# Attention: a pair's query and key copies queued behind the last exponential two pairs ahead, loads half a pair sooner

## The chip, the cores and the metric

The kernel runs on one core of one Trainium2 chip. The metric is the device time of one execution in microseconds (us). The engines are named as the profile names them: PE (TensorE, matrix products), PEld (its weight loads), DVE (VectorE), ACT (ScalarE), POOL (GpSimd) and SP (SyncE, which issues the DMAs here). Each engine works through its own queue in order.

## The reference

A causal attention feeds two mixture-of-experts style layers. Only the attention part is touched by the change.

```
batch, n_heads, seq, head_dim = (2, 12, 448, 64)
scale = 1.0 / np.sqrt(q.shape[-1])
scores = scale * np.matmul(q, k.transpose(0, 1, 3, 2))
mask = np.triu(np.ones((seq, seq), dtype=bool), k=1)
scores = np.where(mask, -1000000000.0, scores)
scores = scores - np.max(scores, axis=-1, keepdims=True)
attn = np.exp(scores)
attn = attn / (np.sum(attn, axis=-1, keepdims=True) + 1e-09)
return np.matmul(attn, v).astype(np.float32)
...
x = np.ascontiguousarray(attn_out.transpose(0, 2, 1, 3)).reshape(B * S, H * D)
x = _moe_ref(x=x, **moe_kwargs)
return _moe2_ref(x=x, **moe2_kwargs)
```

## The kernel before

**Pairs.** The 24 heads are handled as 12 pairs (`units`, numbered `u` from 0): two heads of 64 dimensions fill the 128 partitions. Matrix products keep float32 accuracy by splitting each operand into a high and a low part and adding three products: high by high, high by low, low by high.

**Preparing a pair (`s_prep`, L179).** `kh` is the key's high part (a DVE copy, L62), `kl` its low part (a POOL subtraction, L67). `qs` holds the scaled query, high part from ACT (L60), low part from a DVE instruction (L191, `SCALAR_TENSOR_TENSOR`). From the second pair on, `qs` is then copied by two DMAs on SP's queue (L202, one per head) into the block layout `q` with zeros between the heads. There are two `q` buffers (`qz`), so pair u and pair u+2 share one; three raw buffers `qk` for the loads (`s_load`, L171), and two raw buffers `v` (`load_v`, L177).

**Scores and softmax.** Per pair there are seven chunks of 64 query rows (c = 0 to 6, 64(c+1) key columns). A chunk is three products on PE (L229, tile `s`, four buffers in PSUM), a masked maximum on DVE (L239, tile `mn`) and an exponential on ACT (L242, tile `p`, with row sums). POOL scales `p` by the reciprocal sums (`s_norm`, L246; `rs` is the sums' tile), PE transposes it (L272, tile `pt`), ACT and DVE make its high and low part, PE multiplies by the values (L290, tile `pv`), and ACT and DVE make the high and low part of the result (`xhi`, `xlo`).

**The loop.** The loop over half pairs (k from -3; `u, h = divmod(k, 2)`) writes PE's order out by hand in `products`. An odd half k = 2u+1 holds pair u's transposes 2 and 3, the scores of pair u+2 for the chunks 2, 0, 1, 3 and value products of pair u-1. The even half k = 2u holds the scores of pair u+1 for the chunks 6, 4, 5, pair u's transposes 0 and 1 and value products. So a pair's scores begin with chunk 2 in an odd half and end with chunk 5 in the next even one. On the other engines the order is the scheduler's; `tc.issue_after(x)` tells it to put an instruction behind x. In the kernel before, the preparation of pair u+3 is written in the odd half k = 2u+1, behind the maximum and the exponential of chunk 1 of pair u+2. Near the end of the attention, the first products of the next layer (`pa`, L314 to L316) are mixed in; their weights are converted on DVE (L118 to L122) and POOL.

At the start of the program, `warm` issues dummy products (`wp`, six at first) while the first loads come in.

Of the kernel before, what the change touches and what calls it, by code (L numbers as in the profile page):

```python
# [32 lines left out]
def f32(ap):  # L33
    return ap.bitcast(F32)


CFG = dict(
    first=1, rt5=[1, 3, 4, 5, 8], hp=3000, xe=[1, 7, 8, 10, 12], turn=5, xfd=[3, 4, 5, 6], xfj=[1, 2, 3, 4],
    joint=1, mhi="A", rt6=[1, 4, 7, 9, 15], woh="A", h2h="A", h2l="V", rt=[1, 3, 5, 7, 10], et=[9, 10, 14],
    turn2=[1, 3], ft0=[(0, 3), (1, 3), (2, 3), (3, 3), (4, 3)], ft1=[4], ft2=[3, 5, 6, 7], late=[(2, 5), (3, 5)], ew=[2, 4, 10, 10, 10, 12, 14], stop=0, mlo="V", xh="A", h2="A",  # L40
    wh="G", wil="G", wol="GV", warm=6, nsa=6, nwi=3, nwb=3, wo0=4, hs0=[4, 5, 8, 9], conv0=17, convs=2, pin=1,
    qsb=2, pb=2, ptb=2, qkraw=3, vraw=2, vb=2, ss=4, pts=2, pvs=2, pas=4, wsp=1,
    man=(2, 21),
    ch=(((2, 0, 1), (3,), ()), ((6,), (4, 5), ())), wn=[3, 2, 2], qh="A", qdir=1, qss=2, rpin=5, qdma="SS", kh="V",
    vh="AG", kl="G", vl="G", pth="AAAA", nrm="GGGGGGG", u0=1, order=[2, 1, 3, 0, 4], pm=1,
# [3 lines left out]
def build(tc, qkd, vd, w_in, w_out, emb, tau, wm, cst, out, dbg_y=None):  # L49
    nc = tc.nc  # L50
    V, A, G, T, DMA = nc.vector, nc.scalar, nc.gpsimd, nc.tensor, nc.sync

    ENG = {"A": A, "V": V, "G": G, "S": DMA}
# [4 lines left out]
    def copy_on(eng, out, in_, scale=1.0):  # L58
        if eng is A:
            return A.activation(out, in_, AF.Copy, scale=scale)  # L60
        elif scale == 1.0:
            return eng.tensor_copy(out, in_)  # L62
        else:
            return eng.tensor_scalar(out=out, in0=in_, scalar1=scale, scalar2=None, op0=ALU.mult)

    def lo_of(eng, lo, x, hi):
        return eng.tensor_tensor(out=lo, in0=x, in1=hi, op=ALU.subtract)  # L67
# [18 lines left out]
    ct = cpool.tile([P, cs.shape[1]], F32, name="ct")  # L86
# [41 lines left out]
    last = {}  # L128
# [5 lines left out]
    units = [(b, pr) for b in range(B) for pr in range(NP_)]  # L134
    NU = len(units)
# [24 lines left out]
    def ab(key, u):  # L160
        x = CFG[key]
        return ENG[x[units.index(u) % len(x)]]

    def s_load(u):
        b, pr = u
        qk = apool.tile([P, 2, S], F32, tag="qk", bufs=CFG["qkraw"], name="qk")
        if u == units[0]:
            for i in range(2):
                DMA.dma_start(out=qk[:, i], in_=qkd[b, pr, :, i])
        else:  # L170
            DMA.dma_start(out=qk, in_=qkd[b, pr])  # L171
        st[u] = dict(q=qk[:, 0], k=qk[:, 1])

    def load_v(u):
        b, pr = u
        st[u]["v"] = v = apool.tile([P, NB, P], F32, tag="v", bufs=CFG["vraw"], name="v")
        last["load"] = last["load", units.index(u)] = DMA.dma_start(out=v, in_=vd[b, pr])  # L177

    def s_prep(u):  # L179

        d = st[u]
        for x in ("kh", "kl"):
            d[x] = apool.tile([P, S], F32R, tag=x, bufs=CFG["qsb"], name=x)
        d["q2"] = qz[units.index(u) % len(qz)]
        first = u == units[0] and CFG["u0"]
        kh = copy_on(V if first else ab("kh", u), d["kh"], d["k"])

        def split(r, hi, lo):
            q = d["q"][r].rearrange("p (c a) -> p c a", a=QC)
            copy_on(ENG[CFG["qh"]], hi, q, scale=SCALE)  # L190
            V.scalar_tensor_tensor(out=lo, in0=q, scalar=SCALE, in1=f32(hi), op0=ALU.mult, op1=ALU.subtract)  # L191

        heads = [slice(h * D, (h + 1) * D) for h in range(2)]
        if units.index(u) < CFG["qdir"]:
            with tc.issue_after(kh.ins):
                for h, r in enumerate(heads):
                    split(r, d["q2"][r, :, h, :, 0], d["q2"][r, :, h, :, 1])
        else:
            q = apool.tile([P, NQ, QC, 2], F32R, tag="qs", bufs=CFG["qss"], name="qs")
            split(slice(0, P), q[:, :, :, 0], q[:, :, :, 1])  # L200
            for h, r in enumerate(heads):
                ENG[CFG["qdma"][h]].dma_start(out=f32(d["q2"][r, :, h]), in_=f32(q[r]))  # L202
        lo_of(V if first else ab("kl", u), d["kl"], d["k"], f32(d["kh"]))

    def s_prep_v(u):
        d = st[u]
        d["vh"], d["vl"] = vz[units.index(u) % len(vz)]
        vh, vl = (x[:, :, 0:3:2, :] for x in (d["vh"], d["vl"]))
        v = d["v"].rearrange("p a (h b) -> p a h b", h=2)
        copy_on(ab("vh", u), vh, v)  # L210
        lo_of(V if u == units[0] and CFG["u0"] else ab("vl", u), vl, v, f32(vh))
# [119 lines left out]
    def w_in_load():  # L331
        f = len(wt)
        if f < NF:
            wt[f] = w_load(w_in, f, slots[f % NWI], f"wi{f}", wl="wil", parts=CFG["wsp"] if in_attn else 1)

    def norm_at(k):
        u = (k + 2) // 2
        if 0 <= u < NU:
            s_norm(units[u], sum(CFG["ch"][k % 2], ()))
# [2 lines left out]
    s_load(units[1])  # L342
    load_v(units[0])
    s_load(units[2])
    load_v(units[1])
    s_prep(units[0])


# [4 lines left out]
    def warm(n):  # L353
        for _ in range(n):
            T.matmul(wp, wz[:, 0:P], wz, start=True, stop=True)
# [7 lines left out]
    def half_unit(k):  # L363

        u, h = divmod(k, 2)
        run = {}
        for x in (6, 4, 5) if h == 0 else (2, 0, 1, 3):
            v = u + 1 + h
            if 0 <= v < NU:
                run["s", x] = s_scores(units[v], x)  # L370
        if 0 <= u < NU:
            for i in (0, 1) if h == 0 else (2, 3):
                run["t", i] = trans(units[u], i)
        if 1 <= u <= NU:
            for j, g in ((0, 1), (3, 1), (0, 0), (3, 0)) if h == 0 else ((1, 0), (2, 0), (1, 1), (2, 1)):
                run["v", j, g] = s_pv(units[u - 1], j, g)
        return run
# [7 lines left out]
    def products(k, run):  # L385

        h = k % 2
        if h == 0:
            mix(run, ("s", 6))
            mix(run, ("t", 0))  # L390
            mix(run, ("v", 0, 1), ("v", 3, 1), ("v", 0, 0))
            mix(run, ("s", 4))
            mix(run, ("s", 5))
            mix(run, ("v", 3, 0))
            mix(run, ("t", 1))
        elif k == -3:
            mix(run, *(("s", c) for c in (2, 0, 1, 3)))
        else:
            mix(run, ("t", 2))
            mix(run, ("s", 2))  # L400
            mix(run, ("s", 0), ("v", 1, 0))
            mix(run, ("s", 1), ("v", 2, 0))
            mix(run, ("v", 1, 1))
            mix(run, ("v", 2, 1))
            mix(run, ("t", 3))
            mix(run, ("s", 3))

    man_a = tc.manual_schedule(engines={mybir.EngineType.PE})
    for k in range(-3, 2 * NU + 2):
        u, h = divmod(k, 2)  # L410
        if h == 1 and 3 <= u + 4 < NU:
            s_load(units[u + 4])
        if h == 0 and 0 <= u and u + 2 < NU:
            load_v(units[u + 2])
        if k == 2:
            DMA.dma_start(out=ct, in_=cst)
        while len(wt) < min(NWI, max(0, (k - CFG["conv0"]) // CFG["convs"])):
            if CFG["pin"]:
                with tc.issue_after(last["max"].ins):
                    w_in_load()  # L420
            else:
                w_in_load()
        if k == CFG["man"][0]:
            man_a.__enter__()
        if k == CFG["man"][1]:
            man_a.__exit__(None, None, None)
        if k == -3:
            s_prep(units[1])
        norm_at(k)
        products(k, half_unit(k))  # L430
        if k + 3 < len(CFG["wn"]):
            warm(CFG["wn"][k + 3])
        if (k == -2 or h == 1 and u >= 0) and u + 3 < NU:
            i = max(u + 3, 2)
            x = (0, 3) if i == 2 else (i - 1, 1)
            with tc.issue_after(last["max", *x].ins), tc.issue_after(last["exp", *x].ins):
                s_prep(units[i])
        if h == 1 and 0 <= u + 1 < NU:
            with tc.issue_after(last["max", 0, 5].ins), tc.issue_after(last["exp", 0, 5].ins):
                s_prep_v(units[u + 1])  # L440
# [898 lines left out]
```

## Time and profile before

| | before |
|---|---|
| median of 3 runs | 582.53 us (582.45 to 583.53) |
| the profiled execution | 584.23 us, of which the span from first to last instruction is 582.4 us |
| PE busy | 548.3 us (94%) |
| DVE busy | 401.0 us (69%) |
| ACT busy | 290.2 us (50%) |
| POOL busy | 182.7 us (31%) |
| mean granted PE clock | 0.98 |

The attention takes about the first 125 us of the span. In the rest PE is busy almost without a break. A time in the rows is counted from the start of the span. "Idle before" is the idle time of an engine just before an instruction, with what ended it.

### The profile page before, as it was taken

How to read it: one execution, taken by the hardware profiler on the slowest of the kernel's cores; microseconds unless marked ns; L12 is line 12 of the kernel's file. 1: busy time of each engine (PE TensorE's matmuls, PEld its weight loads, DVE VectorE, ACT ScalarE, POOL GpSimd, SP SyncE). 2: the span in 40 equal slices, each digit the busy share in tenths (PEclk: the TensorE clock that was granted, in tenths of full speed). 3: DMA queues.
4: the chain of work that ended last, by engine and by line, in shares of the span. 5: the costliest groups of instructions: out<-in, count | busy, mean ns of one | idle time of the engine just before them, and what ended most of it. 6: DMA issues, size and time to landing. Idle time of an engine off the chain costs nothing.

```text
span 582.4 us, 9627 instructions
## 1 busy us (share of the span) xinstructions
PE 548.3 (94%) x3427; PEld 511.4 (88%) x3428; DVE 401.0 (69%) x956; ACT 290.2 (50%) x638; POOL 182.7 (31%) x228
## 2 busy tenths in 40 slices
PE   7788786899999999999999999999999999999993
PEld 5687786888899999999999999989998898899992
DVE  6867686596488797779565446798267899883641
ACT  4867576552353524442423331851166888764641
POOL 8747575594463565322100000100210201200010
PEclk9989898799999999999999999999999999999997
DMA  7536534232253544633100002910778789874310
GB/s 233 137 108 218 135 87 95 51 110 99 75 194 130 209 162 163 216 135 140 54 1 29 27 28 87 401 56 2 280 236 282 251 288 333 308 238 175 110 50 6
DMA packets 28234, 86.52 MB, mean 149 GB/s; under 512 B 2822, under 2 KB 13062, under 8 KB 28176
## 3 DMA queue, kind: packets, MB, share of 16 engines
q1 hardware_dynamic: 26640, 79.51, 41.3%
q0 software_dynamic: 1536, 6.29, 3.0%
q8 instruction: 29, 0.48, 0.3%
q14 instruction: 29, 0.24, 0.1%
HBM read 75.24 MB, written 6.29 MB: 140 GB/s over the span
## 4 chain that ended last, share of the span: by engine, by line
PE 83%; DMA 6%; DVE 5%; ACT 2%; issue 2%; SPq 1%; POOL 0%; POOLq 0%; DVEq 0%; ACTq 0%
PE yps L577 19%; PE ops L947 10%; PE pa L314 7%; PE pa L315 7%; PE pa L316 7%; DMA q<-qs 5%; PE pv L290 5%; PE s L229 5%; PE hps L848 3%; PE ops L885 2%; PE ops L880 2%; PE hps L866 2%; PE pt L272 2%; PE hps L868 2%; PE hps L867 2%; DVE ml L67 2%
## 5 line engine op out<-in xcount | busy, mean ns | idle before, releaser
L67 DVE TENSOR_TENSOR ml<-xraw,mh 128x768 fp32r<-128x768 f32 x64 | 59.7, 957 | 10.3 <-ACT mh L60 9.5
L229 PE MATMUL s<-kh,q 128*128 128x128 f32 (+6 forms) x168 | 48.6, 336 | 19.3 <-DMA q<-qs 16.8
L242 ACT ACTIVATE p<-s,mn 128x192 f32<-128x192 f32 (+6 forms) x84 | 39.7, 475 | 34.8 <-DVE mn L239 22.2
L60 ACT ACTIVATE mh<-xraw 128x768 fp32r<-128x768 f32 x64 | 52.2, 843 | 7.6 <-PE ops L880 5.8
L229 PEld LDWEIGHTS s<-kh,q 128*128 128x128 f32 x168 | 35.0, 226 | 23.3 <-issue 11.0
L947 PE MATMUL ops<-mh,act 128*128 128x384 f32 x224 | 53.5, 341 | 0.0
L290 PE MATMUL pv<-pt,v 128*128 128x448 f32 (+7 forms) x288 | 51.8, 314 | 0.0
L239 DVE CUSTOM_DVE_ANT_0 s<-s,maskf 128x192 f32<-128x192 f32 (+6 forms) x77 | 32.1, 432 | 26.8 <-PE s L229 25.8
L255 POOL TENSOR_SCALAR p<-p,rs 128x192 f32<-128x192 f32 (+6 forms) x84 | 43.8, 538 | 17.9 <-DVE rs L251 14.4
L122 DVE SCALAR_TENSOR_TENSOR w<-raw,w 128x768 int32<-128x768 int32 x32 | 43.5, 1363 | 0.7
L290 PEld LDWEIGHTS pv<-pt,v 128*128 128x128 f32 (+1 forms) x288 | 42.1, 177 | 1.7
L973 POOL DMA_INDIRECT out<-osb,fsi x10 | 10.3, 1028 | 99.3 <-ACT osb L968 65.9
L947 PEld LDWEIGHTS ops<-mh,act 128*128 128x128 f32 x224 | 39.2, 188 | 0.8
L67 DVE TENSOR_TENSOR hs<-h,hs 128x512 fp32r<-128x512 f32 (+1 forms) x32 | 21.8, 690 | 23.9 <-ACT hs L60 23.8
L67 DVE TENSOR_TENSOR ml<-mraw,mh 128x768 fp32r<-128x768 f32 x32 | 29.9, 956 | 10.2 <-ACT mh L60 9.8
L120 DVE SCALAR_TENSOR_TENSOR w<-raw,w 128x768 int32<-128x768 int32 x32 | 36.5, 1142 | 0.7
L985 POOL DMA_INDIRECT xr<-ydram,fgi x10 | 10.5, 1051 | 84.1 <-DVE fsi L693 45.4
L67 DVE TENSOR_TENSOR pt<-pt 128x512 fp32r<-128x512 f32 x48 | 32.1, 682 | 4.7 <-ACT pt L60 4.4
L320 ACT ACTIVATE relu<-pa 128x448 f32<-128x448 f32 x32 | 17.0, 539 | 35.3 <-PE pa L316 35.3
L118 DVE TENSOR_SCALAR w<-raw 128x768 int32<-128x768 int32 x32 | 23.7, 741 | 12.2 <-POOL wi3l L67 4.2
L60 ACT ACTIVATE pt<-pt 128x512 fp32r<-128x512 f32 x48 | 28.2, 597 | 7.1 <-PE pt L272 7.1
L272 PE MATMUL pt<-ident,p 128*128 128x128 f32 x192 | 28.9, 282 | 0.8 <-DVE pt L67 0.4
(462 smaller groups left out, 1643.5 us busy)
## 6 DMA issues: line engine op xcount, KB each, us to landing
xraw<-in_wm SPq DMA_DIRECT2D x32, 768.0 KB, 6.8
raw<-in_w_in SPq DMA_DIRECT2D x16, 768.0 KB, 5.1
raw<-in_w_out SPq DMA_DIRECT2D x16, 768.0 KB, 4.0
mraw<-in_wm SPq DMA_DIRECT2D x16, 768.0 KB, 6.5
qk<-in_qkd SPq DMA_DIRECT2D x11, 448.0 KB, 5.0
q<-qs SPq DMA_DIRECT2D x22, 224.0 KB, 3.4
v<-in_vd SPq DMA_DIRECT2D x12, 256.0 KB, 3.1
ydram<-ysb SPq DMA_DIRECT2D x7, 384.0 KB, 2.3
```

The lines of the kernel that those rows point to most:

```text
L60: return A.activation(out, in_, AF.Copy, scale=scale)
L67: return eng.tensor_tensor(out=lo, in0=x, in1=hi, op=ALU.subtract)
L122: V.scalar_tensor_tensor(out=w[:, x], in0=raw[:, x, 0], scalar=29, in1=w[:, x], op0=ALU.logical_shift_right, op1=ALU.bitwise_or)
L229: T.matmul(ss, d["q2"][:, c, :, :, x].rearrange("p a b -> p (a b)"), d[y][:, :n], start=i_ == 0, stop=i_ == 2 and not first)
L255: G.tensor_scalar(out=p, in0=p, scalar1=rs[:, COL[c]:COL[c] + 1], scalar2=1.0, op0=ALU.mult, op1=ALU.mult)
L272: T.transpose(pt[:, o * P:(o + 1) * P], d["p"][c][:, j * P:(j + 1) * P], ident)
L290: T.matmul(d["pv"][:, j * P:S] if h else d["pv"][0:D, j * P:S], d[x][:, j, 1:3].rearrange("p a b -> p (a b)") if h else d[x][:, j, 0], pt[ ...
L314: T.matmul(ps, wh[:, c], xhi[:, kc, gs], start=(kc == 0), stop=False)
L315: T.matmul(ps, wh[:, c], xlo[:, kc, gs], start=False, stop=False)
L316: T.matmul(ps, wl[:, c], xhi[:, kc, gs], start=False, stop=(kc == KC - 1))
L577: T.matmul(ps[t][c][:, :384], x, w[:, c * 384:(c + 1) * 384], start=(f == 0 and w is wh and x is hi), stop=(f == NF - 1 and x is lo))
L947: T.matmul(ps[c], x, ww[:, c * 384:(c + 1) * 384], start=(fc == 0 and x is hh and ww is wh), stop=(fc == 7 and x is hl))
```

## The change

The preparation of pair u+3 is written half a pair sooner: in the even half k = 2u, behind the maximum and the exponential of chunk 5 of pair u+1, which is the last use of the `q` buffer that the new pair takes over. The raw query and key load of pair u+4 moves from the odd half k = 2u+1 to the even half k = 2u. The values of pair 1 and the raw load of pair 3 are put behind the first DMA copies of `qs`; the constants' table `ct` goes from k = 2 to k = 3 and behind the values of pair 3. Eight instead of six dummy products stand at the start.

```diff
-    wh="G", wil="G", wol="GV", warm=6, nsa=6, nwi=3, nwb=3, wo0=4, hs0=[4, 5, 8, 9], conv0=17, convs=2, pin=1,
+    wh="G", wil="G", wol="GV", warm=8, nsa=6, nwi=3, nwb=3, wo0=4, hs0=[4, 5, 8, 9], conv0=17, convs=2, pin=1,
...
-                ENG[CFG["qdma"][h]].dma_start(out=f32(d["q2"][r, :, h]), in_=f32(q[r]))
+                last["q"] = ENG[CFG["qdma"][h]].dma_start(out=f32(d["q2"][r, :, h]), in_=f32(q[r]))
...
     s_load(units[2])
-    load_v(units[1])
     s_prep(units[0])
...
-        if h == 1 and 3 <= u + 4 < NU:
-            s_load(units[u + 4])
-        if h == 0 and 0 <= u and u + 2 < NU:
-            load_v(units[u + 2])
-        if k == 2:
-            DMA.dma_start(out=ct, in_=cst)
+        if k == -2:
+            with tc.issue_after(last["q"].ins):
+                load_v(units[1])
+                s_load(units[3])
+        elif h == 0:
+            if u + 4 < NU:
+                s_load(units[u + 4])
+            if u + 2 < NU:
+                load_v(units[u + 2])
+        if k == 3:
+            with tc.issue_after(last["load", 3].ins):
+                DMA.dma_start(out=ct, in_=cst)
...
-        if (k == -2 or h == 1 and u >= 0) and u + 3 < NU:
-            i = max(u + 3, 2)
-            x = (0, 3) if i == 2 else (i - 1, 1)
+        if h == 0 and u + 3 < NU:
+            x = (0, 3) if u < 0 else (u + 1, 5)
             with tc.issue_after(last["max", *x].ins), tc.issue_after(last["exp", *x].ins):
-                s_prep(units[i])
+                s_prep(units[u + 3])
```

What moves on ACT is seen around the exponentials of one pair in mid-attention (`p1c` is chunk c of an odd pair, `p0c` of the next, even one; `qs` is the high part of a coming pair's query). Before:

```order
L242 ACTIVATE p15_125,sm_734<-s_832,mn_735 128x384
L60 ACTIVATE pt_855<-pt_857 128x512
L242 ACTIVATE p02_115,sm_864<-s_867,mn_865 128x192
L242 ACTIVATE p00_113,sm_864<-s_873,mn_865 128x64
L242 ACTIVATE p01_114,sm_864<-s_882,mn_865 128x128
L60 ACTIVATE qs_915<-qk_718 128x448
```

and now:

```order
L242 ACTIVATE p15_125,sm_745<-s_836,mn_746 128x384
L60 ACTIVATE qs_855<-qk_665 128x448
L60 ACTIVATE pt_866<-pt_868 128x512
L242 ACTIVATE p02_115,sm_875<-s_878,mn_876 128x192
L242 ACTIVATE p00_113,sm_875<-s_884,mn_876 128x64
L242 ACTIVATE p01_114,sm_875<-s_893,mn_876 128x128
```

`qs` stood behind the exponential of the next pair's chunk 1, and stands now right behind the last exponential of the odd pair, with one `pt` copy and three exponentials behind it.

On DVE, at the same place of the program, the low part of `qs` (L191) is the instruction that SP's copies wait for; `ISA s,mn` is a masked maximum, whose number of columns tells the chunk (192 is chunk 2, 64 chunk 0, 128 chunk 1, 256 chunk 3, 448 chunk 6). Before:

```order
L67 TENSOR_TENSOR pt_938<-pt_971,pt_937 128x512
L239 ISA s_1003,mn_995<-s_1003,maskf_127 128x64
L239 ISA mn_995 128x1
L239 ISA s_1012,mn_995<-s_1012,maskf_127 128x128
L239 ISA mn_995 128x1
L62 CAST kh_1042<-qk_848 128x448
L251 RECIPROCAL rs_866<-rs_866 128x3
L67 TENSOR_TENSOR pt_986<-pt_987,pt_985 128x512
L239 ISA s_1036,mn_995<-s_1036,maskf_127 128x256
L239 ISA mn_995 128x1
L191 SCALAR_TENSOR_TENSOR qs_1045<-qk_848,qs_1045 128x448
```

and now:

```order
L239 ISA s_966,mn_876<-s_966,maskf_127 128x384
L239 ISA mn_876 128x1
L62 CAST kh_982<-qk_795 128x448
L251 RECIPROCAL rs_877<-rs_877 128x4
L67 TENSOR_TENSOR pt_942<-pt_975,pt_941 128x512
L239 ISA s_1008,mn_1006<-s_1008,maskf_127 128x192
L239 ISA mn_1006 128x1
L239 ISA s_1014,mn_1006<-s_1014,maskf_127 128x64
L239 ISA mn_1006 128x1
L191 SCALAR_TENSOR_TENSOR qs_985<-qk_795,qs_985 128x448
```

`kh` has moved from behind chunk 1's maximum to behind the last maximum of the pair before, and `qs` from behind chunk 3's maximum (in other pairs before: from behind chunk 1's or chunk 6's) to behind chunk 0's.

On POOL the subtraction `kl` is moved too. Before, around the scaling of one even pair's `p`:

```order
L250 TENSOR_SCALAR rs_866<-sm_864 128x4
L67 TENSOR_TENSOR v11_112<-v_663,v10_111 128x4x2x64
L255 TENSOR_SCALAR p02_115<-p02_115,rs_866 128x192
L255 TENSOR_SCALAR p00_113<-p00_113,rs_866 128x64
L255 TENSOR_SCALAR p01_114<-p01_114,rs_866 128x128
L255 TENSOR_SCALAR p03_116<-p03_116,rs_866 128x256
L250 TENSOR_SCALAR rs_866<-sm_864 128x3
L67 TENSOR_TENSOR kl_1043<-qk_848,kh_1042 128x448
```

and now:

```order
L250 TENSOR_SCALAR rs_877<-sm_875 128x4
L67 TENSOR_TENSOR kl_983<-qk_795,kh_982 128x448
L255 TENSOR_SCALAR p02_115<-p02_115,rs_877 128x192
L255 TENSOR_SCALAR p00_113<-p00_113,rs_877 128x64
L255 TENSOR_SCALAR p01_114<-p01_114,rs_877 128x128
L255 TENSOR_SCALAR p03_116<-p03_116,rs_877 128x256
L250 TENSOR_SCALAR rs_877<-sm_875 128x3
```

`kl`, which needs `kh`, now stands ahead of the scaling of the chunks 2, 0, 1 and 3.

## Rows read from the trace of the kernel before

**Rows 1.** PE's waits from 20 to 126 us: total us, times, longest.

```profile
PE s L229 <- DMA q<-qs: 16.8, 8, 3.4
PE s L229 <- ACT p L242: 1.0, 1, 1.0
```

**Rows 2.** Busy us per engine in stretches: pairs, their sum, start and tail; PEclk is granted clock.

```profile
core 0: us, PE busy (x) PEld busy (x) DVE busy (x) ACT busy (x) POOL busy (x), PEclk, DMA share, GB/s
...
20.55:30.41 9.86, 6.46 (x49) 5.84 (x49) 7.07 (x24) 6.78 (x22) 8.26 (x18) 0.99 0.43 106
30.41:40.42 10.01, 9.26 (x61) 8.85 (x62) 6.49 (x21) 6.35 (x19) 4.78 (x8) 0.84 0.35 80
40.42:49.73 9.31, 7.80 (x61) 7.40 (x62) 6.93 (x22) 7.00 (x23) 5.75 (x9) 1.00 0.48 119
...
60.88:70.84 9.96, 9.33 (x61) 8.91 (x62) 6.00 (x20) 6.08 (x19) 6.22 (x11) 0.83 0.38 88
...
90.35:102.92 12.57, 9.35 (x61) 8.94 (x62) 8.25 (x25) 7.16 (x21) 6.44 (x12) 0.83 0.25 59
102.92:114.43 11.51, 10.46 (x62) 10.05 (x62) 6.12 (x22) 6.55 (x20) 5.65 (x10) 0.75 0.28 63
114.43:130.00 15.57, 15.23 (x103) 14.14 (x104) 14.93 (x32) 8.24 (x23) 13.96 (x19) 1.00 0.29 99
30.41:114.43 84.02, 69.59 (x489) 66.32 (x489) 56.02 (x183) 54.48 (x164) 51.07 (x88) 0.90 0.44 116
```

**Rows 3.** The chain of waits in order of time, 40 to 62 us: start, us, what.

```profile
45.19 0.60 SPq L202
...
45.84 3.80 DMA q<-qs
```

**Rows 4.** PE's instructions in order of time, 46 to 62 us: start, us, what, idle before.

```profile
47.13 1.09 PE L272 MATMUL pt<-ident,p 128*128 128x128 f32 x8
49.73 0.34 PE L229 MATMUL s<-kh,q 128*128 128x192 f32 x1 [1.50 <-DMA q<-qs]
...
60.88 0.40 PE L229 MATMUL s<-kh,q 128*128 128x192 f32 x1 [3.35 <-DMA q<-qs]
```

**Rows 5.** ACT's instructions in order of time, 46.5 to 52 us.

```profile
48.47 0.58 ACT L242 ACTIVATE p<-s,mn 128x384 f32<-128x384 f32 x1
...
49.04 1.07 ACT L60 ACTIVATE pt<-pt 128x512 fp32r<-128x512 f32 x2
```

**Rows 6.** DVE's instructions in order of time, 46.5 to 57 us.

```profile
50.34 0.37 DVE L239 CUSTOM_DVE_ANT_0 s<-s,maskf 128x192 f32<-128x192 f32 x1 [1.97 <-PE s L229]
...
50.71 0.66 DVE L67 TENSOR_TENSOR pt<-pt 128x512 fp32r<-128x512 f32 x1
...
51.37 0.21 DVE L239 CUSTOM_DVE_ANT_0 s<-s,maskf 128x64 f32<-128x64 f32 x1
```

**Rows 7.** The preparation's instructions by tile, 14 to 115 us: ns min/median/max, first and last start.

```profile
L62 DVE CAST kh<-qk x10: 387/390/786, 13.8 to 106.0; 128x448 fp32r<-128x448 f32 x10
L67 POOL TENSOR_TENSOR kl<-qk,kh x10: 1137/1152/1533, 14.7 to 107.9; 128x448 fp32r<-128x448 f32 x10
...
L60 ACT ACTIVATE qs<-qk x9: 607/617/626, 23.0 to 106.6; 128x448 fp32r<-128x448 f32 x9
L191 DVE SCALAR_TENSOR_TENSOR qs<-qk,qs x9: 616/907/1022, 24.3 to 109.2; 128x448 fp32r<-128x448 f32 x9
```

**Rows 8.** Waits of SP's queue from 20 to 115 us: total us, times, longest.

```profile
SPq L202 <- DVE qs L191: 54.6, 8, 10.6
SPq L177 <- POOL v L67: 14.4, 4, 7.3
```

**Rows 9.** PE's first instructions, 0 to 6.5 us.

```profile
1.39 2.74 PE L355 MATMUL wp<-wz 128*128 128x512 bf16 x6 [1.39 <-DVE wz L350]
5.16 1.19 PE L229 MATMUL s<-kh,q 128*128 128x192 f32 x4 [1.02 <-POOL maskf L152]
```

**Rows 10.** The page's costliest groups: one step of a weight conversion on DVE.

```profile
L122 DVE SCALAR_TENSOR_TENSOR w<-raw,w 128x768 int32<-128x768 int32 x32 | 43.5, 1363 | 0.7
```

## The prediction

> **What bounds the kernel now.** I read the waits of PE first, since PE is busy 94% of the span and does almost nothing but wait for a reason or work. In the attention there is one reason: of its idle time from 20 to 126 us, 16.8 us in 8 waits end when a DMA copy `q<-qs` lands; one wait of 1.0 us is for an exponential [rows 1]. All eight stand at the same instruction, the first product of a pair's chunk 2.
>
> Next I cut the trace at these instructions; a "period" is the time from one pair's first product to the next pair's. Eight periods run from 30.41 to 114.43 us, 84.02 us or 10.5 us each, of which PE is busy 69.59 us and idle 14.4 us [rows 2]. In four of them the granted clock is 1.00 and PE is busy 7.79 or 7.80 us (one of the four is shown); the other four, at 0.83, 0.84, 0.83 and 0.75, need 9.26, 9.33, 9.35 and 10.46 us for the same 61 or 62 products [rows 2]. The excess is 7.2 us: after the long waits PE works for a while at the lower of its two levels (1.2 instead of 2.4 GHz). The same product of chunk 2 takes 0.34 us after a wait of 1.50 us and 0.40 us, with slower ones behind it, after one of 3.35 us [rows 4]. So 84.0 = 8 x 7.8 (62.4) + 7.2 + 14.4.
>
> The chain of waits shows what the copy waits for. The first copy is issued at 45.19 us, both have landed at 49.64 us, and PE goes on at 49.73 us: 4.54 us from issue to product [rows 3, 4]. PE had finished the transposes ahead of it at 48.22 us [rows 4]. SP is not late by itself: it waited 54.6 us in 8 waits for the DVE's low part of `qs` [rows 8]. The period is thus a loop: chunk 2's product, chunk 1's exponential, `qs` on ACT and DVE, copy, the next pair's chunk 2. No other engine is full: per period DVE is busy 7.0 us, ACT 6.8, POOL 6.4 (56.02, 54.48 and 51.07 us over eight) [rows 2].
>
> **The change part by part.**
>
> *Preparation half a pair sooner.* It removes no instruction and adds none; it moves 1 ACT, 2 DVE, 1 POOL instruction and 2 copies per pair. The copies for pair u+3 now hang on chunk 5 of pair u+1, and their user comes two periods T after that pair's first product. From the pair that begins at 40.42 us: its last exponential ends at 49.05 us, 8.63 us after its first product [rows 2, 5]. Behind it now come `qs` on ACT, 0.62 us [rows 7]; the `pt` high part, half of 1.07, 0.54 us [rows 5]; on DVE the `pt` low part 0.66, the maxima of chunks 2 and 0, 0.37 and 0.21 us [rows 6]; the low part of `qs`, 0.62 to 1.02 us [rows 7]; then 4.54 us of copy. The sum is 16.2 to 16.6 us, so 2T must be at least that: T of 8.1 to 8.3 us. I allow for a little queueing that this sum leaves out and take T = 8.5 us. Bounds: PE's own 7.8 us below, and above 9.3 us, the shortest period that the copies gave so far (9.31) [rows 2].
>
> What goes if no period waits any more: 16.8 + 1.0 us of waits and 7.2 us of slow clock, 25.0 us. What comes back: 8 x (8.5 - 7.8) = 5.6 us, all of it in gaps of 0.7 us, shorter than the 1.50 us after which PE still ran at full clock. In the stretch before the first long wait (20.55 to 30.41 us, where 3.4 us of the 16.8 lie) PE is busy only 6.46 us but POOL 8.26 us [rows 2]; I give back 0.4 us there.
>
> *The `kl` subtraction ahead of the scaling on POOL*, 1.15 us [rows 7]. It waits for `kh`, which now comes behind the last maximum, and four scalings wait behind it. Their users, the next transposes, come about half a period later, so I cost it at nothing; if that cover is gone it is 1.15 us per period, which stays within T of 9.3 us.
>
> *Loads half a pair sooner, values of pair 1 and the table later.* Each load is an issue on SP's queue ahead of copies. SP has spare time [rows 8]; a load waits for POOL at most 7.3 us in the trace, a wait that then ended without holding a copy. I cost them at nothing, with a rival below for the other case.
>
> *Two more dummy products.* Six take 2.74 us, so two take 0.9 us; PE idles 1.02 us just behind them for POOL [rows 9]. Nothing is paid; uncovered it would be 0.9 us.
>
> *The tail.* From 114.43 to 130 us PE is busy 15.23 of 15.57 us, with DVE at 14.93 and POOL at 13.96 [rows 2]: PE fills its gaps with products of the next layer. PE's order is the scheduler's there, and in the changed kernel several transposes and value products stand ahead of such fillers. They can wait for a DVE that is full. I charge one step of a weight conversion, 1.4 us [rows 10]; bounds are nothing and two steps, 2.7 us.
>
> Sum: 25.0 - 5.6 - 0.4 - 1.4 = 17.6 us. From the profiled execution's 584.23 us this gives 566.6; that one lies 1.7 us above the median of the runs shown, and the prediction is for the median: 582.5 - 17.6 = 564.9 us.
>
> **A rule that speaks against it.** With the gaps gone, DVE and POOL work side by side more. In the trace the same instructions spread: `kh` from 0.39 to 0.79 us, the low part of `qs` from 0.62 to 1.02, `kl` from 1.14 to 1.53 [rows 7]. The Trainium skill, "SBUF — State Buffer", section "SBUF: two separate sides", says that DVE and GpSimd share a pair of ports as an exclusive lock, so that the later one waits for the whole instruction. The spread agrees with it. By that rule the excess would be paid in most periods, which is the first rival.
>
> **The rivals.**
>
> *DVE and POOL in each other's way.* The spread of three instructions is 0.4 us each. If the two on DVE are paid in every period, T grows from 8.5 to about 9.3 at worst; I take 9.0. For it: the spread. Against it: the periods of now already hold a share of it. The gain is 25.0 - 8 x 1.2 - 0.4 - 1.4 = 13.6 us: 568.9 us.
>
> *The copies stay last.* If `qs` on DVE sits so long behind maxima and `pt` that it is hardly sooner, T stays at 9.3, the change not doing what it says, apart from the long waits. For it: the instruction has moved only by two or three places on DVE in some pairs. Against it: it no longer stands behind chunk 3's product. The gain is 25.0 - 8 x 1.5 - 0.4 - 1.4 = 11.2 us: 571.3 us.
>
> *PE alone bounds it.* T = 7.9 and nothing lost in the tail: 25.0 - 0.8 - 0.2 = 24.0 us: 558.5 us. For it: every other engine needs 7.0 us or less per period.
>
> *Slower: POOL's queue holds SP's.* POOL stands at `kl` until `kh` is there, its value low part `v` (the one SP waited up to 7.3 us for) comes later, the value load that waits for it stands ahead of the next copies on SP, and these are late again. POOL has 6.4 us of work, so this decides only once it stands idle more than 4 us per period, giving T above 10.5. At T = 10.7, with the first wait back and the tail's 1.4 us: 8 x 0.2 + 1.4 = 3.0 us more, 585.5 us. Against it: before `kl`, POOL should stand still only from chunk 3's sum to the last maximum.
>
> **How the numbers follow.** Forecast (T from 8.1 to 8.8): 0.50. Ports: 0.20. Copies still last: 0.12. PE alone: 0.12. Slower: 0.04. The rest, 0.02, is no change. The range reaches from PE alone (558.5, so 558) to a little beyond the case of the copies (571.3, with the tail's other 1.3 us: 573). A change under 0.2% (1.2 us) can't be told from none: faster 0.94, same 0.02, slower 0.04.
>
> **What would show it.** PE's waits for `q<-qs` fall from 16.8 us to under 6 us; the granted clock from 30 to 110 us is 1.00; periods are 8.1 to 8.8 us with PE busy 7.8 us in each; the copies are issued two or more us ahead of PE's need minus 4.5. From the tail on, the stretches are as long as before, shifted. I am wrong if the copies still end most periods, if waits for ACT, DVE or POOL take the freed time (periods above 9), or if the tail loses more than 3 us.

## The result, and the profile after

The changed kernel takes 567.64 us (median of 4 runs, 567.15 to 569.09) where the kernel before took 583.03 us (median of 4 runs beside them, 582.45 to 584.15). The ratio is 0.9738, with a 95% interval from 0.9713 to 0.9763: 15.4 us gained where 17.6 us were predicted (564.9 us). The profiled execution of the changed kernel took 569.09 us, its span is 567.4 us, and the mean granted clock is 0.986.

PE's waits from 14 to 130 us; [rows 1] has the kernel before from 20 us on (total us, times, longest):

```profile
PE s L229 <- DMA q<-qs: 5.3, 3, 3.1
PE pt L272 <- POOL p L255: 3.0, 3, 2.3
PE pv L290 <- ACT pt L60: 0.6, 1, 0.6
PE pt L272 <- DVE pt L67: 0.5, 1, 0.5
```

From 20 us on, eight waits for the copies (16.8 us) have become two (4.1 us); the third one above is at 13.85 us. A wait for POOL that the kernel before did not have is new.

The stretches from one pair's first product to the next, as in [rows 2]; the first is the one before the eight periods, the last but one all eight together, the last the beginning of the tail:

```profile
core 0: us, PE busy (x) PEld busy (x) DVE busy (x) ACT busy (x) POOL busy (x), PEclk, DMA share, GB/s
22.78:32.03 9.25, 9.25 (x52) 8.84 (x50) 6.72 (x22) 5.94 (x20) 5.72 (x14) 0.65 0.55 143
32.03:39.59 7.56, 7.56 (x65) 7.36 (x63) 6.78 (x24) 6.70 (x22) 5.71 (x9) 1.00 0.52 123
39.59:48.40 8.81, 7.80 (x65) 7.39 (x63) 7.69 (x25) 7.66 (x24) 7.52 (x12) 1.00 0.63 161
48.40:59.32 10.92, 7.80 (x62) 7.39 (x62) 7.10 (x23) 7.71 (x23) 7.90 (x17) 1.00 0.87 253
59.32:68.42 9.10, 9.10 (x61) 8.89 (x62) 6.28 (x22) 4.83 (x16) 3.79 (x6) 0.81 0.46 115
83.54:91.74 8.20, 7.75 (x64) 7.41 (x63) 7.39 (x25) 7.07 (x22) 6.54 (x12) 1.00 0.52 123
32.03:99.30 67.27, 62.70 (x491) 60.53 (x490) 55.59 (x184) 53.36 (x164) 52.06 (x88) 0.97 0.55 141
99.30:115.00 15.70, 15.46 (x116) 14.34 (x115) 15.30 (x37) 9.95 (x28) 13.23 (x19) 1.00 0.40 120
```

Four of the eight periods take 7.56 us, and PE has no gap in them (one is shown, the others begin at 68.42, 75.98 and 91.74). The other four are those of 8.81, 10.92, 9.10 and 8.20 us. In the period of 9.10 us PE is busy all the time, but at a granted clock of 0.81; the first stretch is like it, at 0.65.

The same cuts in both kernels show where the time came from. "Predicted" is worked out from the prediction's terms: the start holds the first wait of 3.4 us less the 0.4 us charged there; eight periods at 8.5 us are 68.0; the tail was charged 1.4.

| us | before | after | difference | predicted |
|---|---|---|---|---|
| start of the span to the first of the eight periods | 30.41 | 32.03 | +1.6 | -3.0 |
| eight periods | 84.02 | 67.27 | -16.8 | -16.0 |
| from there to the end of the span | 468.0 | 468.1 | +0.1 | +1.4 |
| sum | 582.4 | 567.4 | -15.0 | -17.6 |

So the eight periods together gained about what was forecast (by luck, as is shown below), the tail cost nothing, and the start went the wrong way by 4.6 us.

**The start.** POOL's instructions in order of time (start, us, what, idle before):

```profile
15.07 0.61 POOL L62 CAST v<-v 128x512 fp32r<-128x512 f32 x1 [4.67 <-DMA v<-in_vd]
15.66 1.96 POOL L255 TENSOR_SCALAR p<-p,rs 128x192 f32<-128x192 f32 x4
17.59 1.29 POOL L67 TENSOR_TENSOR v<-v,v 128x512 fp32r<-128x512 f32 x1
18.83 1.14 POOL L67 TENSOR_TENSOR kl<-qk,kh 128x448 fp32r<-128x448 f32 x1
19.94 1.84 POOL L255 TENSOR_SCALAR p<-p,rs 128x448 f32<-128x448 f32 x3
```

POOL stands 4.67 us at the conversion of pair 1's values, because their load is now issued behind the first copies; the scalings of `p` are queued behind it. PE's instructions in order of time show who pays (and two of the later places):

```profile
1.39 3.60 PE L354 MATMUL wp<-wz 128*128 128x512 bf16 x8 [1.39 <-DVE wz L349]
5.16 0.78 PE L229 MATMUL s<-kh,q 128*128 128x192 f32 x4 [0.17 <-POOL maskf L152]
...
21.27 0.33 PE L272 MATMUL pt<-ident,p 128*128 128x128 f32 x1 [2.30 <-POOL p L255]
...
48.40 0.34 PE L229 MATMUL s<-kh,q 128*128 128x192 f32 x1 [1.01 <-DMA q<-qs]
...
59.32 0.34 PE L229 MATMUL s<-kh,q 128*128 128x192 f32 x1 [3.12 <-DMA q<-qs]
```

The transposes of pair 0 wait 2.30 us for a scaling, pair 2 begins at 22.78 us where it began at 20.30, and the granted clock of the stretch behind it is 0.65.

**The long periods.** SP's queue in order of time:

```profile
42.33 1.27 SPq L202 DMA_DIRECT2D q<-qs  x2
43.64 0.81 SPq L171 DMA_DIRECT2D qk<-in_qkd  x1
...
46.41 0.91 SPq L113 DMA_DIRECT2D raw<-in_w_in  x2
50.98 1.27 SPq L202 DMA_DIRECT2D q<-qs  x2
```

The `raw<-in_w_in` are two weight loads of the next layer, 768 KB each. In the kernel before they were issued at 48.44 us and the next copies at 56.07 us, 7.6 us later; now the copies follow after 4.6 us. The copies issued at 42.33 us, which the first long period waits for, stand ahead of these loads. The DMA issues from 40 to 60 us (out<-in, count, KB each, median us from issue to landing):

```profile
raw<-in_w_in SPq DMA_DIRECT2D x2, 768.0 KB, 9.3
q<-qs SPq DMA_DIRECT2D x4, 224.0 KB, 5.3
```

Over 40 to 62 us of the kernel before, the same two figures are 5.6 and 3.4 us, each from one recorded landing. In the chain of waits the copy issued there comes to 7.57 us:

```profile
42.97 5.33 DMA q<-qs
...
51.62 7.57 DMA q<-qs
```

PE waits 3.12 us for it, and the next period is the slow one.

### The profile page after: what moved, and what is told of

It is laid out like the page before. It is cut to its first block, busy times and chain, and to the rows that moved or that the text cites. A ratio compares the mean times of both kernels' runs of the same rounds, so it can differ in the third digit from the quotient of the medians.

```text
span 567.4 us, 9637 instructions
## 1 busy us (share of the span) xinstructions
PE 542.6 (96%) x3429; PEld 506.5 (89%) x3430; DVE 398.6 (70%) x956; ACT 288.9 (51%) x638; POOL 180.1 (32%) x228
## 4 chain that ended last, share of the span: by engine, by line
PE 84%; DVE 7%; DMA 3%; ACT 3%; POOL 1%; issue 1%; SPq 0%; POOLq 0%; DVEq 0%; ACTq 0%
PE yps L581 19%; PE ops L951 10%; PE pa L314 7%; PE pa L316 7%; PE pa L315 7%; PE pv L290 5%; PE s L229 4%; PE hps L852 3%; PE pt L272 3%; PE ops L889 2%; PE ops L884 2%; DMA q<-qs 2%; PE hps L870 2%; PE hps L872 2%; PE hps L871 2%; DVE ml L67 2%
## 5 line engine op out<-in xcount | busy, mean ns | idle before, releaser
L229 PE MATMUL s<-kh,q 128*128 128x128 f32 (+6 forms) x168 | 45.3, 317 | 6.5 <-DMA q<-qs 5.3
L290 PE MATMUL pv<-pt,v 128*128 128x448 f32 (+7 forms) x288 | 49.0, 304 | 0.7 <-ACT pt L60 0.6
L290 PEld LDWEIGHTS pv<-pt,v 128*128 128x128 f32 (+1 forms) x288 | 39.7, 169 | 2.8 <-ACT pt L60 0.8
L229 PEld LDWEIGHTS s<-kh,q 128*128 128x128 f32 x168 | 32.1, 208 | 9.0 <-issue 5.0
L118 DVE TENSOR_SCALAR w<-raw 128x768 int32<-128x768 int32 x32 | 22.5, 704 | 13.8 <-POOL wi3l L67 4.3
```

What stands on the lines that cost most here:

```text
L229: T.matmul(ss, d["q2"][:, c, :, :, x].rearrange("p a b -> p (a b)"), d[y][:, :n], start=i_ == 0, stop=i_ == 2 and not first)
L290: T.matmul(d["pv"][:, j * P:S] if h else d["pv"][0:D, j * P:S], d[x][:, j, 1:3].rearrange("p a b -> p (a b)") if h else d[x][:, j, 0], pt[ ...
```

## The experiments

All ratios are to the kernel before, run beside the kernel on the same chip. First question: are the two waits (the values at the start, the weight loads at 50 us) really what is left, and does taking one away pay?

**The changed kernel again**, unedited, as a measure for the others.

> The changed kernel once more, on the chip and among the rounds of the next three, so that they can be set beside it. Expected: 567 to 569 us, ratio to the kernel before 0.972 to 0.976. If the long landing of the copies around 51 us belongs to one profiled execution only, it should be missing here; if it is the rule, PE again waits about 3 us for the copy at about 59 us.

567.8 us (564.49 to 569.0, 6 runs), ratio 0.9708 (0.968 to 0.9737). Both places recur: PE waits 2.29 us for POOL at 20.40 us and 2.5 us for the copies at 57.49 us. One kernel's runs spread over 4.5 us, so differences between two variants of under some 2 us are not told apart below.

**Pair 1's values loaded early again.**

```diff
     s_load(units[2])
+    load_v(units[1])
...
-                load_v(units[1])
```

> The changed kernel, but with the load of pair 1's values back at its old place, ahead of the first copies. Theory A (POOL stood 4.67 us for these values and PE's transposes behind it): POOL's wait is gone, PE's waits for POOL of 3.0 us before 23 us are gone, pair 2's first product comes at about 20.3 instead of 22.8 us, and the time falls by 2 to 3.5 us, to about 565 us. Rival B (the early values slow the first copies on the DMA engines, which was why they were moved): the first copies land later by a us or more and the time does not fall, 567 to 569 us.

566.62 us (565.71 to 567.49), ratio 0.9687 (0.9663 to 0.9711). POOL's wait at the start is gone:

```profile
9.68 0.60 POOL L62 CAST v<-v 128x512 fp32r<-128x512 f32 x1
```

Pair 2 begins at 20.78 us, 2.0 us earlier; in place of the waits for POOL, PE now waits 1.88 us for pair 2's own copies. In this trace the gain is eaten at the next place. The copies are now issued at 46.63 us, 3.3 us behind the weight loads (43.28), take 8.97 us, and PE waits longer than in the changed kernel:

```profile
56.37 0.50 PE L229 MATMUL s<-kh,q 128*128 128x192 f32 x1 [4.55 <-DMA q<-qs]
```

**The two weight loads later**, behind a later pair's raw load.

```diff
-    ... qss=2, rpin=5, ...
+    ... qss=2, rpin=9, ...
```

> The changed kernel, but with the first two weight loads of the next layer (768 KB each) pinned behind the values of pair 9 instead of pair 5, so that they are issued at about 85 us instead of 46 us. Theory A (these loads share the DMA engines with the copies issued at 42 and 51 us and stretch their landing to 6 and 8 us): both copies land within 4.5 to 5 us of their issue, PE's waits of 1.0 and 3.1 us go, the slow clock of the pair behind (1.5 us) goes too, and the time falls by 4 to 5.5 us, to about 563 us. Rival B (it is the raw query and key load, or SP's queue, that holds the copies): the waits stay, 567 to 569 us. Rival C: the copies at 85 to 95 us are stretched instead and the wait only moves, or the weights come too late for the tail: 565 to 570 us.

566.29 us (563.22 to 568.73), ratio 0.9688 (0.9658 to 0.9718). The two periods that were 10.92 and 9.10 us are 7.55 and 7.56 us now, so these loads were what stretched the copies that the first of them ended with. The period of 8.81 us stays: it is 8.79 us here (36.44 to 45.23 us), and its copy takes as long as in the changed kernel, with no weight load near it. From the chain of waits and from PE:

```profile
39.83 5.31 DMA q<-qs
```

```profile
45.23 0.34 PE L229 MATMUL s<-kh,q 128*128 128x192 f32 x1 [0.98 <-DMA q<-qs]
```

So something else stretches that copy. And the collision has moved with the loads, as SP's queue and PE show:

```profile
76.14 1.57 SPq L113 DMA_DIRECT2D raw<-in_w_in  x2
78.05 1.36 SPq L202 DMA_DIRECT2D q<-qs  x2
```

```profile
87.33 0.34 PE L229 MATMUL s<-kh,q 128*128 128x192 f32 x1 [2.97 <-DMA q<-qs]
```

The period behind this wait takes 7.55 us at a granted clock of 1.00.

**Both edits together.**

> Both edits in one kernel: pair 1's values early and the weight loads behind pair 9's values. If both theories hold and the two don't touch each other: 6 to 9 us less than the changed kernel, 559 to 562 us, periods of 7.6 to 8.2 us from pair 3 to pair 11. If the wait only moves from one place to the next (a rival for either), less than 3 us.

564.21 us (563.12 to 569.93), ratio 0.9669 (0.9631 to 0.9707), short of the 559 to 562 us expected. The weight loads stand ahead of copies here too (issued at 76.74 and 77.22 us, a copy at 78.72 that lands in 6.94 us). Waits that the profile puts down to copies are down to 3.2 us in 3, none over 1.2; a wait of 1.85 us for a `pt` copy on ACT came up at 86.89 us, which I did not follow further.

Next question: which part of the change brings the gain? **The preparation alone**, in the kernel before, with all loads, the table and the dummy products as they were.

```diff
-        if (k == -2 or h == 1 and u >= 0) and u + 3 < NU:
-            i = max(u + 3, 2)
-            x = (0, 3) if i == 2 else (i - 1, 1)
+        if h == 0 and u + 3 < NU:
+            x = (0, 3) if u < 0 else (u + 1, 5)
...
-                s_prep(units[i])
+                s_prep(units[u + 3])
```

> The kernel before with the preparation alone moved (loads, table and dummy products as before). The theory that the earlier preparation carries the gain: 564 to 568 us; pair 1's values are then still loaded ahead of the first copies, so POOL's stall at the start is missing too, and pair 2 begins at about 20.5 us. Rival (the preparation needs the earlier raw loads, which take 5 us to land): ACT and DVE wait for the raw load in most periods, and the time stays at 572 us or more.

566.19 us (563.65 to 567.61), ratio 0.9688 (0.9663 to 0.9712): the whole gain. Pair 2 begins at 20.30 us as before. The weight loads stand 3.4 us ahead of copies here too:

```profile
42.80 0.91 SPq L113 DMA_DIRECT2D raw<-in_w_in  x2
46.16 1.27 SPq L202 DMA_DIRECT2D q<-qs  x2
```

```profile
55.50 0.50 PE L229 MATMUL s<-kh,q 128*128 128x192 f32 x1 [4.15 <-DMA q<-qs]
```

**Everything but the preparation**: the changed kernel with the edit above undone.

> The changed kernel with the preparation back at its old place, so that only the loads, the table and the two dummy products are moved. The theory: the copies bound every period as before, PE waits 15 to 17 us for them, and pair 1's late values cost up to 2.5 us at the start: 583 to 587 us. Rival (a good part of the gain came from the earlier loads): 575 us or less.

586.49 us (582.92 to 589.22, 12 runs), ratio 1.0032 (1.0008 to 1.0056), a little slower. The copy loop stands as in [rows 1], and the wait for POOL at the start is there:

```profile
PE s L229 <- DMA q<-qs: 14.4, 8, 3.6
PE pt L272 <- POOL p L255: 2.3, 2, 2.0
```

Last question: can the collision be taken away instead of moved? **The two weight loads one by one, each right behind a pair's copies** (those of pairs 8 and 9), so that some 6 us lie between each load and the next copies.

```diff
-    ... qss=2, rpin=5, ...
+    ... qss=2, rpin=8, ...
...
-        with tc.issue_after(last.get(("load", CFG["rpin"]), last["load"]).ins):
+        with tc.issue_after(last.get(("qc", CFG["rpin"] + f), last["load"]).ins):
...
-                last["q"] = ENG[CFG["qdma"][h]].dma_start(out=f32(d["q2"][r, :, h]), in_=f32(q[r]))
+                last["q"] = last["qc", units.index(u)] = ENG[CFG["qdma"][h]].dma_start(out=f32(d["q2"][r, :, h]), in_=f32(q[r]))
```

> The changed kernel with the first two weight loads one by one, each pinned directly behind a pair of copies (pairs 8 and 9) and not behind a value load. Theory A (the copies' landing is stretched by whatever large load was issued in the few us ahead of them): the raw loads are through before the next copies are issued, no copy takes over 6 us to land, PE's waits for copies sum to under 2 us and the time falls by 3 to 5 us, to 563 to 565 us. Rival (any extra load costs the same wherever it stands, as the time of the last batch with the loads behind pair 9's values suggests): 566 us or more.

563.86 us (562.0 to 566.58), ratio 0.9648 (0.9623 to 0.9673). No wait for a copy is over 1.2 us, though they sum to 4.1 us where under 2 were expected; a period of 8.84 us (from 39.97 us) is still there. What is left besides is the start's wait for POOL:

```profile
PE s L229 <- DMA q<-qs: 4.1, 5, 1.2
PE pt L272 <- POOL p L255: 3.2, 4, 2.3
```

**That, and pair 1's values early.**

> The same, and pair 1's values early. Theory A: about 2 us less than the last one, 561 to 563 us, the best of all. Rival: no better than the earlier pairing of the two edits, 564 us.

561.67 us (558.67 to 562.87), ratio 0.9606 (0.9581 to 0.963). Three pairs of kernels now differ in the place of this load alone: 567.8 and 566.62 us, 566.29 and 564.21, 563.86 and 561.67. Loading the values early gains 1.2, 2.1 and 2.2 us, each near the least that can be told apart, all three the same way. Of the waits for copies (3.9 us in 3), 2.4 us are at pair 2's own copies, which lie behind two raw loads and take 8.8 us to land.

**The preparation alone, and the weight loads behind copies**; all other loads as in the kernel before.

> The kernel before with two edits: the preparation moved, and the two weight loads one by one behind the copies of pairs 8 and 9. All other loads, the table and the dummy products stand as before. Theory (the two are all that counts; moving the other loads only hurts at the start): pair 2 begins at about 20.3 us without a wait for its copies, no copy takes over 6 us, PE waits for copies under 3 us in all, 559 to 561.5 us. Rival (from the middle of the attention on the earlier raw loads do help): 562 us or more.

561.85 us (556.79 to 563.26), ratio 0.9611 (0.9573 to 0.9648); the execution in the trace took 558.14. From 20 to 96 us PE waits for no copy at all:

```profile
PE pt L272 <- DVE pt L67: 0.7, 2, 0.5
PE s L229 <- ACT p L242: 0.2, 1, 0.2
```

The copies from 12 to 125 us land in 3.3 us at least, 3.8 in the median and 4.9 at most (in the changed kernel 3.2, 3.8 and 7.6), though the two weight loads are issued at 61.26 and 68.74 us, 1.6 and 0.7 us behind a copy. The eight periods together:

```profile
26.69:88.21 61.52, 60.81 (x491) 58.94 (x489) 54.84 (x184) 52.19 (x165) 53.30 (x90) 1.00 0.61 157
```

That is 7.69 us each at full clock.

**The one before it again**, beside this one.

> The best kernel of the last batch once more, among the same rounds: 560 to 562.5 us, pair 2 begins at about 21.6 us after a wait of some 2 us for its copies.

561.41 us (559.6 to 562.45), ratio 0.9618 (0.959 to 0.9646). Pair 2 begins at 19.94 us after a wait of 0.94 us, where the run before had 21.63 and 2.4 us: the start differs between executions of one kernel. The two versions are not told apart. Both beat the kernel before by 3.8 to 3.9% and the changed kernel by about 1%; the one without the moved loads is the smaller edit.

## Why the prediction was right, and where its sizes were not

**The waits for copies go because the copies are queued sooner: shown.** With this edit alone the ratio is 0.9688, without it 1.0032. The eight periods average 8.41 us where T = 8.5 was taken. That the two meet is luck: where nothing stretches the copies a period takes 7.56 us, 0.9 less than was taken, and nearly all of that was lost again to waits and a slow clock that the sum did not have. The forecast's own signs tell as much: the waits and the tail came out as named, but the granted clock is 0.97 and not 1.00, and of the eight periods only the one of 8.20 us lies between 8.1 and 8.8.

**T itself is composed otherwise than the sum had it.** The sum of 16.2 to 16.6 us laid ACT's and DVE's work behind the last exponential end to end. ACT's and DVE's instructions in order of time, for the pair that begins at 32.03 us:

```profile
39.92 0.58 ACT L242 ACTIVATE p<-s,mn 128x384 f32<-128x384 f32 x1
...
40.48 0.63 ACT L60 ACTIVATE qs<-qk 128x448 fp32r<-128x448 f32 x1
```

```profile
40.48 0.69 DVE L67 TENSOR_TENSOR pt<-pt 128x512 fp32r<-128x512 f32 x1
...
41.48 0.77 DVE L191 SCALAR_TENSOR_TENSOR qs<-qk,qs 128x448 fp32r<-128x448 f32 x1
```

The exponential ends 8.47 us after the pair's first product (8.63 was taken). The copies are issued at 42.33 us, 1.83 us later, where the sum had 3.0 to 3.4: DVE did its `pt` while ACT made the high part of `qs`. With 4.54 us for the copy the loop needs 14.8 us in two periods, T = 7.4, less than PE's own work. PE's own work is also less than the 7.8 us taken as its floor: four periods of 7.56 us without a gap. So where nothing stretches the copies, the rival "PE alone bounds it" is what happens; two periods leave 15.12 - 10.30 = 4.8 us from issue to product.

**What makes 8.41 of 7.56 is a step that the prediction did not have.** It took 4.54 us for every copy and did not ask which loads would now be issued just ahead of one. The copy issued at 50.98 us gives the 10.92 us period, and the slow clock behind its wait the 9.10: together 4.9 of the 6.8 us by which eight periods exceed 8 x 7.56. That the 768 KB loads stretch this copy is shown by moving them: the wait left there and came up where they went, and with the loads right behind copies it is gone.

The period of 8.81 us has another cause, which stays open. The copy issued at 42.33 us serves a product at 48.40, 6.07 us later: 1.25 us over the 4.8, the whole excess of this period. The weight loads were issued only behind it, at 46.41 us, and with them moved away its period is still 8.79 us.

The period of 8.20 us pays 0.45 us for the preparation itself. On DVE the low part of `qs` now stands ahead of the `pt` that PE's next transposes wait for (read from the order, not tried); DVE's and PE's instructions:

```profile
84.67 0.94 DVE L191 SCALAR_TENSOR_TENSOR qs<-qk,qs 128x448 fp32r<-128x448 f32 x1
...
85.67 0.68 DVE L67 TENSOR_TENSOR pt<-pt 128x512 fp32r<-128x512 f32 x1
```

```profile
86.50 0.63 PE L272 MATMUL pt<-ident,p 128*128 128x128 f32 x4 [0.45 <-DVE pt L67]
```

On the weight loads, the Trainium skill, "DMA: Bandwidth & Descriptors", section "Two DMAs through the same engine are not ordered", says that within one queue of one DMA engine descriptors start in order. The traces agree: the copy queued behind the weight loads landed in 7.57 us, and in the kernel with the preparation alone and the loads queued 1.6 and 0.7 us behind copies, these copies land in 3.8 us. No run puts the copies on another queue, so it is not shown that the order in the queue alone does it.

**Slow clock, 7.2 us: forecast to go, did not quite.** Of the periods one is at 0.81, 1.5 us over 7.56, behind the longest wait. The stretch ahead of the periods is at 0.65: PE is busy 9.25 us in it, where the kernel before did the same 52 products in 6.71 busy us, 2.5 less:

```profile
20.30:30.41 10.11, 6.71 (x52) 6.09 (x51) 7.25 (x26) 7.03 (x23) 8.38 (x18) 0.99 0.44 114
```

**"Values of pair 1 ... later", costed at nothing: this step failed.** The search for who waits went to SP's queue, which had spare time and still has; the wait was on POOL, in whose queue the conversion of these values stands ahead of the scalings that PE needs. It set pair 2 back by 2.5 us (20.30 to 22.78), and with the low clock behind it the start is 4.6 us worse than forecast, more than the whole error of 2.6 us in the span. With the load put back, POOL's wait is gone. Of the 4.6 us the three pairs of kernels show 1.2 to 2.2 as this load's price. The rest is not shown to be: with the values late, the first of the eight periods begins at 32.03, 30.89, 28.88 and 32.41 us in four traces (changed kernel, the same again, weight loads late, weight loads behind copies), with the start's loads issued in the same order in all four.

**`kl` ahead of the scaling, at nothing: right.** POOL stands about 1 us per period at `kl` (6.9 us in 7 waits from 20 to 100 us, which the profile ends at PE's transposes and not at `kh`), and no product waits for it in the periods.

**Two more dummy products, nothing paid: right.** Eight take 3.60 us, the idle time behind them shrinks from 1.02 [rows 9] to 0.17 us, and the first product starts at 5.16 us in both kernels.

**The tail, 1.4 us: not paid.** 0.1 us, the lower bound.

**The rival of DVE and POOL in each other's way: not seen.** With fewer gaps the three instructions of [rows 7] spread less, not more:

```profile
L62 DVE CAST kh<-qk x9: 384/389/743, 20.1 to 91.4; 128x448 fp32r<-128x448 f32 x9
...
L67 POOL TENSOR_TENSOR kl<-qk,kh x10: 1134/1150/1158, 18.8 to 92.0; 128x448 fp32r<-128x448 f32 x10
...
L191 DVE SCALAR_TENSOR_TENSOR qs<-qk,qs x9: 620/655/937, 25.2 to 93.3; 128x448 fp32r<-128x448 f32 x9
```

The median of the low part of `qs` fell from 0.907 to 0.655 us. The rule that was weighed against the change does not show its price here.

**POOL's queue holding SP's: not seen.** SP's waits for the values' low part fell from 14.4 [rows 8] to 9.3 us, and SP's longest such wait from 7.3 to 3.7. Its waits for POOL's `rs` ahead of the value load rose from 2.1 to 9.0 us, so SP waits for POOL no less there; but no copy is held by it, for SP still waits at the copies for DVE's low part of `qs` (39.7 us in 9 waits). The risk was on POOL's queue, but its head was pair 1's values, not `kl`.

**What stays open.** Why copies with no weight load ahead of them take 3.8 us in most periods and 5.3 in some (the period of 8.81 us is one) stays unexplained. The raw loads beside them are an obvious suspect, but two traces speak against them: with the values early a copy issued at 39.85 us lands in 3.79 us, with the weight loads late one issued at 39.83 us takes 5.31, and both have a value load some 4 us ahead of the first copy and a raw load 0.7 us behind the second. Which of the two best versions is faster is not settled.

## What to carry to other kernels

Where a DMA copy closes a loop, look not only at when it is issued but at what was issued in the few microseconds ahead of it: here 1.5 MB of weight loads doubled the time of a 224 KB copy, and moving the preparation is what brought the two together. A load that is moved later has to be followed to the engine that converts it, and to everything queued there behind the conversion; spare time on the issuing queue says nothing about that. And work of two engines behind one event is not a sum end to end: lay it out engine by engine before taking it as a bound. An average that meets the forecast proves none of its terms: look at the periods one by one.

## What the runs showed of the hardware that was not expected

The 224 KB copy from `qs` to `q` landed in 3.2 us at best and in 8.97 us when issued 3.3 us behind two 768 KB loads. A period's 7.8 us of busy PE, with gaps, became 7.56 us without gaps for the same work: busy time that the profile models is no exact floor. The length of a wait did not tell the clock behind it: in the changed kernel a wait of 2.30 us at 21.27 us stood before a stretch at a granted clock of 0.65 and one of 3.12 us before 0.81, while with the weight loads late a wait of 2.97 us left the next period at 1.00.
